# Batch 0 in half units of 256 and 320 tokens, with tiles of 64 tokens of two heads on 128 partitions

## The chip, the cores and the metric

The kernel runs on one core of a Trainium2 chip. The metric is the device time of one execution in microseconds. Five engines work side by side, each through its own list of instructions in order: TensorE (PE, with its weight loads as PEld), VectorE (DVE), ScalarE (ACT), GpSimd (POOL) and SyncE (SP), which issues most transfers.

## The reference, cut to what matters

```python
# q, k, v: (4, 8, 576, 64); M_prev: (4, 8, 64, 64); z_prev: (4, 8, 64); beta: (8,)
scores = q @ k.T / 8; scores[j > i] = -1e9
a = exp(scores - scores.max(-1)); a /= a.sum(-1) + 1e-09
local = a @ v
q_p = where(q > 0, q, exp(q) - 1) + 1
mem_out = (q_p @ M_prev) / ((q_p * z_prev).sum(-1) + 1e-6)
g = 1 / (1 + exp(-beta))
x = (g * mem_out + (1 - g) * local)          # to (2304 tokens, 512)
h = maximum(x @ w_in1, 0);  x = (s * h * h + b) @ w_out1
h = x @ w_in2;              out = (h * tanh(softplus(h))) @ w_out2
```

The attention is causal over 576 tokens of each batch, with a memory term. Two feed-forward layers of 512 x 2048 x 512 follow. The weights come as 64-bit numbers and are converted on the chip.

## The kernel before, in words

**A planner.** The program lists steps (`Plan.add`), each with an engine, an estimated duration, a priority, the buffers that it reads, writes or holds, and a function that issues the instructions. `Plan.order` runs an event simulation over these estimates and so fixes the order of the instructions of every engine; of the steps that are ready on an engine, the one with the lowest priority number goes first. A step that starts a buffer waits until its ring has a free place. The attention's TensorE steps carry a mode (1 for scores, 2 for the product with v), and among ready steps those of the current mode go first. Every transfer of attention and weights is a step of SP's queue.

**Attention in half units** (`pair`, from line 477). A half unit is a pair of heads (p = 0 to 3) of one batch and one group of tiles of 128 tokens: group TA (tiles 0 to 2, whose first 64 rows are padding: 320 tokens) or TB (tiles 3 and 4: 256 tokens). Batch 0's eight half units have priorities 7 x p for TA and 28 + 5 x p for TB (constants TIME_A, FIRST_B, TIME_B); the others start at 50. In one half unit, in the order of the list:

- transfers: q and z in rows (lines 514 to 517), q and k transposed (lines 521 and 524), M and v (line 656). A TA half of batch 0 keeps them in one of the four feed-forward weight buffers with r = 3, which aren't needed yet;
- the feature map: min with 0 on GpSimd (line 535), exp on ScalarE (536), max-add (537), product with z (538) and sum over 64 columns (539) on VectorE, then a gate (533) and a reciprocal (541) per row;
- scores on TensorE (line 571): contraction over 64 rows, so the two heads stand in the two row halves of the array;
- per tile and head: mask, row minimum of the negated scores on VectorE (line 581), the memory row q_p x gate of 64 columns on GpSimd (592), exp with row sums on ScalarE (589);
- gate and reciprocal of the row sums (533, 610), scaling of each tile (607; all on VectorE for batch 0's TA; for the rest tile 3 on GpSimd and tile 4 on VectorE);
- transposes on TensorE in blocks of 128 columns (line 630), copied from PSUM by ScalarE (635);
- the product PV with [M; v] on TensorE (line 652), contraction over 128 and each head in one column half. A batch-0 TA half then writes 256 tokens as a high and a low part straight into the first feed-forward block's input (lines 663 and 664), and every half copies its tokens (666) and stores them in `x_d` (668).

All PSUM results of the attention share the ring "a" of five banks.

**Weights.** `convert` takes one piece of 128 x 512 of a weight (of 64 pieces in the two layers, 32 in the first): a transfer of 512 KB (line 702), two ScalarE steps (707 and 713), a VectorE step that joins the bits (717), and the split into a high and a low part (724 and 727, both on VectorE). The constants CONV give each group of four pieces its priorities. `raw_buf` gives each piece one of a few landing buffers, some of them weight buffers that are not in use yet.

**The first feed-forward layer** goes in blocks of 256 tokens, with priority from 500 (RANK1), below all of the attention. Line 881 is its first product, line 957 the second. Block 0 needs `first_x` of all four TA halves; block 1 loads tokens 256 to 511 back from `x_d` (`load_x`, lines 902 to 904), which `x_needed` ties to the halves that cover them. Until the first matmul of line 881, the planner puts products of zeros (line 1389) where TensorE would be idle:

```python
    plan.fill = (7.0, 85.0, 0.12, zero_product)
    plan.fill_end = in_steps[0][0]
```

The half units and their places are listed near the end:

```python
    halves_ = [(0, p, TA, TIME_A * p, (nm, NR - 1), p % 2) for p, nm in enumerate(("wih", "wil", "woh", "wol"))]
    halves_ += [(0, p, TB, FIRST_B + TIME_B * p, x, p % 2) for p, x in enumerate((("woh", 2), ("wol", 2), ("wih", 3), ("wil", 3)))]
    for b, p, g, prio, *x in halves_[:H]:
        pair(b, p, prio, g, *x)
```

## Time and profile before

| | us |
|---|---|
| runs, median of 3 | 957.2 (957.04 to 958.82) |
| the profiled execution, its own time | 956.4 |
| its span, from first to last instruction | 954.6 |
| TensorE busy | 937.3 |
| VectorE busy | 776.0 |
| ScalarE busy | 641.5 |
| GpSimd busy | 220.7 |

How to read it: the profile is one execution recorded by the hardware profiler. Busy times are unions over an engine's instructions, so neighbouring instructions that overlap are not counted twice; the length given for a group of several instructions runs from the first start to the last end. Ends of matmuls are modelled. An idle time is put down to what released the instruction that ended it. The granted TensorE clock was 1.00 of full speed in all stretches.

### The profile page before, as it was taken

To read this page: it belongs to the slowest core of one execution; us is meant where nothing else is said; L and a number is where in the kernel's file an instruction comes from. 1 tells how busy PE (TensorE), PEld (TensorE's weight loads), DVE (VectorE), ACT (ScalarE), POOL (GpSimd) and SP (SyncE) were. 2 spreads that over 40 slices of the span, in tenths; PEclk is the share of its full clock that TensorE was granted. 3 is DMA by queue.
4 is the path that set the end of the run, shared out by engine and by line. 5 is a ranking of instruction groups with operands and counts; after the bars stand their busy time and mean duration, and the time that the engine had idled before them with its cause. 6 is when DMAs were issued, how large, how long until landed. Compare 5 with 4: busy or idle time off the path is not lost.

```text
span 954.6 us, 19318 instructions
## 1 busy us (share of the span) xinstructions
PE 937.3 (98%) x6594; PEld 862.0 (90%) x6594; DVE 776.0 (81%) x1886; ACT 641.5 (67%) x1393; POOL 220.7 (23%) x377
## 2 busy tenths in 40 slices
PE   7899999999999999999999999999999999999998
PEld 6677788878788999888899999999999999999998
DVE  6999989899978787568658998889957799577874
ACT  6899878777777476889757865557634476344652
POOL 4635445577663000000023400000000000000000
PEclk9999999999999999999999999999999999999999
DMA  9976757999996789988885658885786655775545
GB/s 236 311 201 176 235 162 224 266 267 265 283 257 198 221 282 308 291 301 274 291 289 165 206 184 266 303 278 177 234 285 218 209 163 191 259 226 199 170 139 178
DMA packets 148339, 224.11 MB, mean 235 GB/s; under 512 B 15120, under 2 KB 122640, under 8 KB 141328
## 3 DMA queue, kind: packets, MB, share of 16 engines
q1 hardware_dynamic: 141408, 174.63, 59.4%
q0 software_dynamic: 6688, 48.24, 15.3%
q8 instruction: 52, 0.85, 0.4%
q14 instruction: 47, 0.39, 0.1%
q10 hardware_dynamic: 144, 0.00, 0.0%
HBM read 159.39 MB, written 63.44 MB: 233 GB/s over the span
## 4 chain that ended last, share of the span: by engine, by line
PE 79%; DVE 4%; ACT 2%; DMA 1%; issue 1%; POOL 0%; DVEq 0%; POOLq 0%
PE bank L1112 20%; PE bank L1185 19%; PE bank L881 12%; PE bank L957 12%; PE bank L1188 5%; PE bank L652 4%; PE bank L630 4%; PE bank L571 3%; DMA stage<-wi_sums_d 1%; DVE S L740 1%; DMA qn<-in_qz 0%; DVE g L1118 0%; DVE woh L740 0%; POOL Pt L607 0%; DVE g L1150 0%
## 5 line engine op out<-in xcount | busy, mean ns | idle before, releaser
L1112 PE MATMUL bank<-wi,woh 128*128 128x384 f32 x477 | 112.5, 334 | 0.0
L1112 PE MATMUL bank<-wi,wol 128*128 128x384 f32 x483 | 105.9, 335 | 0.8 <-DVE wil L1118 0.6
L1185 PE MATMUL bank<-wol,S 128*128 128x256 f32 x756 | 102.3, 283 | 0.0
L1185 PE MATMUL bank<-woh,S 128*128 128x256 f32 x756 | 101.9, 283 | 0.0
L1185 PEld LDWEIGHTS bank<-wol,S 128*128 128x128 f32 x756 | 96.2, 192 | 0.0
L1185 PEld LDWEIGHTS bank<-woh,S 128*128 128x128 f32 x756 | 95.9, 192 | 0.0
L1112 PEld LDWEIGHTS bank<-wi,wol 128*128 128x128 f32 x483 | 85.6, 188 | 1.6 <-DVE wil L1118 0.9
L1112 PEld LDWEIGHTS bank<-wi,woh 128*128 128x128 f32 x477 | 85.2, 188 | 0.4
L589 ACT ACTIVATE Pt<-Pt,mx 128x64 f32<-128x64 f32 (+4 forms) x152 | 82.6, 564 | 1.8 <-DVE mx L581 1.8
L635 ACT COPY PT<-bank 128x384 f32<-128x384 f32 (+2 forms) x160 | 68.2, 491 | 22.4 <-PE bank L630 15.0
L607 POOL TENSOR_SCALAR Pt<-Pt,rs 128x448 f32<-128x448 f32 (+3 forms) x100 | 65.7, 676 | 39.2 <-DVE rs L610 26.8
L592 POOL TENSOR_SCALAR Pt<-ex,nm 128x64 f32<-128x64 f32 x152 | 60.2, 419 | 63.1 <-DVE nm L541 35.4
L630 PE MATMUL bank<-ident,Pt 128*128 128x128 f32 x444 | 62.5, 275 | 6.1 <-DVE Pt L607 1.7
L630 PEld LDWEIGHTS bank<-ident,Pt 128*128 128x128 f32 x444 | 49.5, 140 | 11.2 <-issue 3.4
L581 DVE CUSTOM_DVE_ANT_0 Pt<-bank,mask 128x64 f32<-128x64 f32 (+3 forms) x152 | 50.5, 373 | 8.0 <-PE bank L571 5.7
L739 ACT CAST woh<-stage 128x1024 fp32r<-128x1024 f32 (+2 forms) x42 | 37.2, 885 | 27.4 <-PE bank L1112 17.9
L740 DVE TENSOR_TENSOR woh<-stage,woh 128x1024 fp32r<-128x1024 f32 (+2 forms) x42 | 42.7, 1018 | 13.8 <-ACT woh L739 13.7
L1125 POOL TENSOR_SCALAR woh<-woh,sb 128x384 f32<-128x384 f32 (+1 forms) x6 | 5.5, 916 | 183.3 <-ACT woh L1124 183.3
L739 ACT CAST S<-g 128x384 fp32r<-128x384 f32 x56 | 28.7, 513 | 27.2 <-PE bank L1185 19.2
L1092 POOL DMA_DIRECT2D woh<-wo_split_d x13 | 6.9, 530 | 156.2 <-DVE g L1150 76.4
L881 PE MATMUL bank<-xh,wi 128*128 128x256 f32 x256 | 42.5, 292 | 0.0
L957 PE MATMUL bank<-gl,woh 128*128 128x256 f32 x256 | 41.5, 288 | 0.0
(331 smaller groups left out, 2491.1 us busy)
## 6 DMA issues: line engine op xcount, KB each, us to landing
woh<-wo_split_d POOLq DMA_DIRECT2D x13, 1024.0 KB, 5.6
wol<-wi_split_d POOLq DMA_DIRECT2D x12, 1024.0 KB, 5.2
wol<-wo_split_d POOLq DMA_DIRECT2D x11, 1024.0 KB, 5.2
stage<-in_w_in SPq DMA_DIRECT2D x21, 512.0 KB, 5.6
stage<-in_w_out SPq DMA_DIRECT2D x19, 512.0 KB, 4.7
stage<-wi_d SPq DMA_DIRECT2D x24, 384.0 KB, 5.1
stage<-wo_d SPq DMA_DIRECT2D x18, 512.0 KB, 3.7
wo_split_d<-high SPq DMA_DIRECT2D x32, 256.0 KB, 4.6
```

The costliest lines, as they stand in the source:

```text
L581: nc.vector.tensor_tensor_reduce(at_t(i, t, D + lo, D + hi), x.t[:, a:a + hi - lo], mask[:, SP - w + lo:SP - w + hi], -SCALE, mx.t[:, i, t ...
L589: nc.scalar.activation(at_t(i, t, D, w + D), at_t(i, t, D, w + D), AF.Exp, bias=mx.t[:, i, t + k:t + k + 1], scale=-1.0, accum_out=rs.t[:, ...
L592: add(POOL, 0.33, lambda i=i, t=t: nc.gpsimd.tensor_scalar(at_t(i, t, 0, D), ex.t[:, i, t - lo_t, :], nm.t[:, i, t - lo_t:t - lo_t + 1], 1 ...
L607: (nc.vector if e == DVE else nc.gpsimd).tensor_scalar(x, x, r, *((None, ALU.mult) if e == DVE else (1.0, ALU.mult, ALU.mult)))
L630: nc.tensor.transpose(ps.t[:, x, :], at_t(i, t, c * P, (c + 1) * P), ident)
L635: (nc.vector.tensor_copy if dve else nc.scalar.copy)(PT[i].t[:, x:x + n], ps.t[:, :n])
L739: lambda: (nc.scalar.copy if e == ACT else nc.vector.tensor_copy)(t[0](0), src()), r, [t[2], half], after)
L740: lo = two(add(DVE, dve_us(n), prio, lambda: nc.vector.tensor_tensor(t[0](1), src(), t[0](0).bitcast(F32), op=ALU.subtract), [*r, half], [ ...
L881: nc.tensor.matmul(ph, w_at(nm, r, cc)[:, o:o + P], x_at(x, cc), start=(begin and part == 0 and cc == 0), stop=(part == 2 and cc == NCC - ...
L957: nc.tensor.matmul(acc[ec // per].t[:, (ec % per) * n:(ec % per + 1) * n], w_at(nm, fc // FPR, fc % FPR)[:, ec * P:(ec + 1) * P], t(x)[:, ...
L1112: nc.tensor.matmul(ps.t[:, :H2], w[i // 4].t[:, j, kk, at_], x[kk].t[:, k], start=begin and part == kk == 0, stop=part == 2 and kk == 1, s ...
L1185: nc.tensor.matmul(acc[t].t[:, :DH], s.t[:, j, t * P:(t + 1) * P], x.t[:, k, q % 4], start=q == part == 0, stop=q == NQ2 - 1 and part == 2)
```

## The change

Batch 0's eight half units are no longer made by `pair` but by a new function `packed`. The first half has 256 tokens instead of 320, the second 320 instead of 256. In each there is one tile or two whose 128 partitions hold 64 tokens of one head and the same 64 tokens of the other: in the first half tokens 0 to 63 (width 64) and 192 to 255 (width 320, the last 64 keys masked), with one full tile per head between them (tokens 64 to 191); in the second half tokens 256 to 319, with two full tiles per head. Score products of a packed tile are 64 x 64 (line numbers as in the diff), those of a full tile 64 x 128 as before. A second half uses all five banks for scores in two turns, where before it used four.

q and z of the packed tiles and of the first halves are loaded for all pairs by `load_few` into one buffer, in rows of 64 numbers (256 bytes) per descriptor; second halves load the rest of their q. A table `gates` and a mask `steps` for the packed tiles are made at the start. Priorities change: first halves 6 x p, second ones 22 + 5 x p, the other batches from 44, the weight groups behind the first 2 to 4 earlier. The weight pieces with r < 2 use other landing buffers: four for r = 0, three for r = 1 (four before). The first half writes `x_d` up to token 256.

```diff
-TIME_A, FIRST_B, TIME_B, FIRST, TIME = 7.0, 28.0, 5.0, 50.0, 7.0
-CONV = ((-1.0, 3.0), (24.0, 2.0), (32.0, 2.0), (40.0, 2.0), (50.0, 3.0), (62.0, 3.0), (74.0, 3.0), (86.0, 3.0))
+TIME_A, FIRST_B, TIME_B, FIRST, TIME = 6.0, 22.0, 5.0, 44.0, 7.0
+CONV = ((-1.0, 3.0), (22.0, 2.0), (30.0, 2.0), (38.0, 2.0), (46.0, 3.0), (58.0, 3.0), (70.0, 3.0), (82.0, 3.0))
...
+E_PACKED = ('DDDD', 'PPDPD')
...
+    gates = at.tile([P, 2, H // 2, 6], F32, name="gates")
+    nc.vector.tensor_copy(gates[:, :, :, 2:].rearrange("p k a (h t) -> p (k a) h t", t=2),
+                          igate.rearrange("p k (a h) -> p (k a) h", h=2).unsqueeze(3).to_broadcast([P, H, 2, 2]))
+    for i in range(2):
+        x = slice(D * i, D * i + D)
+        nc.vector.tensor_copy(gates[x, :, :, :2], igate[x, :, i::2].unsqueeze(3).to_broadcast([D, 2, H // 2, 2]))
+    steps_ = at.tile([P, 3 * P], BF16, name="steps")
+    nc.gpsimd.memset(steps_[:, :2 * P], 0.0)
+    for i in range(2):
+        x = slice(D * i, D * i + D)
+        nc.gpsimd.tensor_copy(steps_[x, 2 * P:2 * P + D], mask[x, SP - P + D * i:SP - P + D * i + D])
+    nc.gpsimd.memset(steps_[:, 2 * P + D:], MASKED)
...
+    few, few_q, few_z, few_d = Buf(R["wih", 2], [P, 2048]), Buf(), Buf(), Buf()
+
+    def few_at(lo, n, *, s=1, rows=slice(0, P)):
+        return few.t[rows, lo:lo + n * D].rearrange("p (a s d) -> p a s d", s=s, d=D)
+
+    def load_few():
+        def get(us, prio, w, f):
+            attention_steps.append(add(DMA, us, prio, f, w=[w], keep=[few]))
+
+        def half_rows(i):
+            return slice(D * i, D * i + D)
+
+        for i in range(2):
+            for k in range(2):
+                get(0.25, 0.2, few_q, lambda i=i, k=k: nc.sync.dma_start(
+                    few_at(0, 16, s=4, rows=half_rows(i))[:, :, k], qz[0, i::2, (D, 0)[k]:(P, D)[k], (1, 3)[k]].rearrange("h p d -> p h d")))
+        for p in range(H // 2):
+            get(0.25, 0.3 + TIME_A * p, few_q if p == 0 else few_b[p], lambda p=p: nc.sync.dma_start(
+                few_at(0, 16, s=4)[:, p, 2:], qz[0, 2 * p:2 * p + 2, :, 2].rearrange("h p d -> p h d")))
+        get(0.5, 0.6, few_z, lambda: nc.sync.dma_start(few_at(16 * D, 8)[:, :, 0], qz[0, :, :, 0].rearrange("h p d -> p h d")))
+        for i in range(2):
+            get(0.15, 0.6, few_z, lambda i=i: nc.sync.dma_start(
+                few_at(24 * D, 4, rows=half_rows(i))[:, :, 0], qz[0, i::2, half_rows(i), 0].rearrange("h p d -> p h d")))
+        for i in range(2):
+            get(0.15, FIRST_B - 4.0, few_d, lambda i=i: nc.sync.dma_start(
+                few_at(28 * D, 4, rows=half_rows(i))[:, :, 0], qz[0, i::2, D:, 3].rearrange("h p d -> p h d")))
+
+    few_b = [few_q, *(Buf() for _ in range(3))]
...
+    def packed(p, half, prio, place, apart):
...
+        lo = half == 0
+        hs = slice(2 * p, 2 * p + 2)
+        nk, nb, n_s = (320, 3, 4) if lo else (S, 5, 5)
+        nq = 320
+        QN = nq + nk
+        VX = QN + (0 if lo else n_s * D)
+        all_, qk_in, q_in, v_in = Buf(R[place], [P, 2048]), Buf(), Buf(), Buf()
+        slots = (((0, 64), (192, 320), (64, 192, 0), (64, 192, 1)) if lo else
+                 ((0, 320), (64, 448, 0), (192, 576, 0), (64, 448, 1), (192, 576, 1)))
...
+        def q_all():
+            if lo:
+                return few_at(0, 16, s=4)[:, p]
+            return all_.t[:, QN:QN + n_s * D].rearrange("p (s d) -> p s d", d=D)
+
+        z_pair, z_both = (lambda: few_at(24 * D, 4)[:, p]), (lambda: few_at(16 * D + 2 * p * D, 2)[:, :, 0])
+
+        def fetch(us, f, w):
+            add(DMA, us, f, w=[w], keep=[all_])
+
+        if not lo:
+            fetch(0.5, lambda: nc.sync.dma_start(q_all()[:, 1:].rearrange("p (h t) d -> p h t d", t=2), qz[0, hs, :, 4:6].rearrange("h p a d -> p h a d")), q_in)
+        for i in range(2):
+            def load(i=i):
+                src = qk[0, 2 * p + i, rows(i)]
+                if lo:
+                    nc.sync.dma_start(all_.t[rows(i), :2 * nq].rearrange("p (a b) -> p a b", a=2),
+                                      src[:, D:][:, :2 * S].rearrange("p (a b) -> p a b", a=2)[:, :, :nq])
+                else:
+                    nc.sync.dma_start(all_.t[rows(i), :nq + nk], src[:, D + 256:SP + S])
+
+            fetch(0.0009 * (nq + nk), load, qk_in)
...
+        have = [few_q, few_b[p]] if lo else [q_in]
+        keep = [few] if lo else [all_, few]
+        if not lo:
+            add(POOL, 0.3 + 0.0032 * D, lambda: nc.gpsimd.tensor_copy(q_all()[:, 0], few_at(28 * D, 4)[:, p, 0]), [few_d], [q_in], keep)
+        add(POOL, 0.3 + 0.0032 * n_e, lambda: nc.gpsimd.tensor_scalar_min(ex.t, q_all(), 0.0), have, [ex], keep)
+        add(ACT, act_us(n_e), lambda: nc.scalar.activation(ex.t, ex.t, AF.Exp), [ex], [ex])
+        two(add(DVE, dve_us(n_e), lambda: nc.vector.scalar_tensor_tensor(ex.t, q_all(), 0.0, ex.t, op0=ALU.max, op1=ALU.add), [ex, *have], [ex], keep))
+        weighed = Buf()
+        for a, n in ((0, 2), (2, 2)) if lo else ((0, 1), (1, 4)):
+            def weigh(a=a, n=n):
+                x, y = q_all()[:, a:a + n], ex.t[:, a:a + n]
+                z = z_pair().to_broadcast([P, n, D]) if a == 0 else z_both()
+                if n == 4:
+                    x, y = (u.rearrange("p (h t) d -> p h t d", t=2) for u in (x, y))
+                    z = z.unsqueeze(2).to_broadcast([P, 2, 2, D])
+                nc.vector.tensor_tensor(x, y, z, op=ALU.mult)
+
+            two(add(DVE, dve_us(n * D), weigh, [ex, few_z, *have], [weighed], keep))
+        add(DVE, dve_us(n_e), lambda: nc.vector.tensor_reduce(nm.t[:, :n_s], q_all(), axis=mybir.AxisListType.X, op=ALU.add), [weighed], [nm], keep)
...
+        bank, scored = [Buf(R["a"], [P, 512]) for _ in range(2 if lo else 5)], Buf()
+        if lo:
+            where = {0: [(0, 64, 1, 192)], 1: [(0, 320, 0, 192)], 2: [(0, 192, 0, 0)], 3: [(0, 192, 1, 0)]}
+            turns = [([0, 1], [(2, 0, 0), (3, 0, 1), (1, 0, 0), (0, 0, 1), (0, 0, 0), (1, 0, 1)], 832)]
+        else:
+            where = {0: [(0, 320, 4, 0)], **{1 + 2 * i: [(0, 448, i, 0)] for i in range(2)},
+                     **{2 + 2 * i: [(0, 64, i, 448), (64, 576, 2 + i, 0)] for i in range(2)}}
+            turns = [([4, 0, 1], [(0, 0, 0), (3, 0, 1), (1, 0, 0), (0, 0, 1), (4, 0, 1), (2, 0, 0)], 832), ([2, 3], [(2, 1, 0), (4, 1, 1)], 512)]
+        for used, products, columns in turns:
+            def mm(products=products):
+                for s, k, i in products:
+                    q0, w, *full = slots[s]
+                    a, b, x, o = where[s][k]
+                    n = P if full else D
+                    nc.tensor.matmul(bank[x].t[:, o:o + b - a] if full else bank[x].t[rows(i), o:o + b - a],
+                                     all_.t[rows(i), q0:q0 + n], all_.t[rows(i), nq + a:nq + b], start=True, stop=True, skip_group_check=not full)
+
+            add(PE, 0.03 + columns * 0.00167, mm, [qk_in], [*(bank[x] for x in used), scored], [*(x for x, _ in Pt), mx, rs, all_], 1.0)
+            attention_steps[-1].mode = 1
+        for s in (0, 2, 3, 1) if lo else (0, 1, 3, 2, 4):
+            w, full = slots[s][1], len(slots[s]) > 2
+            for k, (a, b, x, o) in enumerate(where[s]):
+                def least(s=s, k=k, a=a, b=b, x=x, o=o, w=w, full=full):
+                    m = mask[:, SP - w + a:SP - w + b] if full else steps_[:, {(0, 64): 2 * P, (192, 320): D, (0, 320): 0}[slots[s]]:][:, :w]
+                    nc.vector.tensor_tensor_reduce(at(s, D + a, D + b), bank[x].t[:, o:o + b - a], m, -SCALE,
+                                                   mx.t[:, s:s + 1] if k else HUGE, ALU.add, ALU.min, mx.t[:, s + 8 * k:s + 8 * k + 1])
+
+                add(DVE, 0.14 + 0.00105 * (b - a), least, [bank[x]] + [mx_in[s]] * k, [Pt_in[s], mx_in[s]], [Pt[s][0], mx])
+            add(POOL, 0.33, lambda s=s: nc.gpsimd.tensor_scalar(at(s, 0, D), ex.t[:, s], nm.t[:, s:s + 1], 1.0, op0=ALU.mult, op1=ALU.mult),
+                [ex, nm], [Pt_in[s]], [Pt[s][0]])
+            add(ACT, 0.28 + 0.00083 * w, lambda s=s, k=k, w=w: nc.scalar.activation(
+                at(s, D, D + w), at(s, D, D + w), AF.Exp, bias=mx.t[:, s + 8 * k:s + 8 * k + 1], scale=-1.0, accum_out=rs.t[:, s:s + 1]),
+                [Pt_in[s], mx_in[s]], [Pt_in[s], rs_in[s]], [Pt[s][0], mx, rs])
...
+        for s in (0, 1, 2, 3) if lo else (0, 1, 3, 2, 4):
+            e, w = on(E_PACKED[half][s]), slots[s][1]
...
+        PT = [Buf(R["PT"], [P, 9, P]) for _ in range(1 if lo else 2)]
+        if lo:
+            groups = [(PT[0], 0, [(0, 0), (1, 0), (1, 1), (1, 2)]), (PT[0], 4, [(2, 0), (2, 1), (3, 0), (3, 1)])]
+        else:
+            groups = [(None, 0, [(0, c) for c in range(3)])]
+            groups += [(PT[i], 0, [(1 + 2 * i, c) for c in range(4)]) for i in range(2)]
+            groups += [(PT[i], 4 + a, [(2 + 2 * i, c) for c in range(a, b)]) for a, b in ((0, 3), (3, 5)) for i in range(2)]
...
+        def mm():
+            for c in range(nb):
+                for k in range(2):
+                    for i in range(2):
+                        x = pv.t[rows(i)]
+                        if lo and k == 0 and c == 0:
+                            dest, src = x[:, :384].rearrange("p (k n) -> p k n", k=2)[:, :, :D], PT[0].t[:, 0:2, rows(i)]
+                        elif lo and k == 0:
+                            dest, src = x[:, 192:256], PT[0].t[:, 1 + c, rows(i)]
+                        elif lo and c < 2:
+                            dest, src = x[:, 64:192], PT[0].t[:, 4 + 2 * i + c]
+                        elif not lo and k == 0 and c < 3:
+                            dest, src = x[:, :D], turned()[:, c, rows(i)]
+                        elif not lo and k == 1 and c < 4:
+                            dest, src = x[:, 64:320].rearrange("p (k n) -> p k n", k=2), PT[i].t[:, c:c + 5:4]
+                        elif not lo and k == 1:
+                            dest, src = x[:, 192:320], PT[i].t[:, 8]
+                        else:
+                            continue
+                        nc.tensor.matmul(dest, v_at(i, c), src, start=c == 0 and k == 0, stop=c == (2, nb - 1 - lo)[k], skip_group_check=k > 0)
...
+        if r < 2:
+            i = k % (4 - r)
+            return Buf(R["raw"], [P, 1024], I32) if i < 2 else Buf(R[("wil", 2) if i == 2 else ("wol", 1)], [P, 2048], I32)
...
-        edge = len(TA) * P - D
-        return [x_in[b, g] for b in range(B) for g in range(2) if b * S + g * edge < t0 + n and b * S + (edge, S)[g] > t0]
+        edge = [N1 if b == 0 else len(TA) * P - D for b in range(B)]
+        return [x_in[b, g] for b in range(B) for g in range(2) if b * S + g * edge[b] < t0 + n and b * S + (edge[b], S)[g] > t0]
...
+    load_few()
     for b, p, g, prio, *x in halves_[:H]:
-        pair(b, p, prio, g, *x)
+        packed(p, int(g == TB), prio, *x)
```

## Rows read from the trace of the kernel before

**Rows 1.** The page: busy time of each engine, and the chain that ended last
```profile
PE 937.3 (98%) x6594; PEld 862.0 (90%) x6594; DVE 776.0 (81%) x1886; ACT 641.5 (67%) x1393; POOL 220.7 (23%) x377
...
PE 79%; DVE 4%; ACT 2%; DMA 1%; issue 1%; POOL 0%; DVEq 0%; POOLq 0%
```

**Rows 2.** TensorE in order of time: start, us, what, count [idle before <-releaser]
```profile
9.20 3.26 PE L571 MATMUL bank<-wih 64*128 64x64 f32 x12 [3.46 <-DMA wih<-in_qk]
...
19.16 1.52 PE L652 MATMUL bank<-PT,wih 128*64 128x384 f32 x12
20.60 1.36 PE L571 MATMUL bank<-wil 64*128 64x64 f32 x12
...
29.08 0.82 PE L630 MATMUL bank<-ident,Pt 128*128 128x128 f32 x6
...
30.54 1.58 PE L652 MATMUL bank<-PT,wil 128*64 128x384 f32 x12
...
45.77 1.52 PE L652 MATMUL bank<-PT,wol 128*64 128x384 f32 x12
...
47.77 2.10 PE L571 MATMUL bank<-wol 64*128 64x448 f32 x12
49.80 1.22 PE L881 MATMUL bank<-xh,wi 128*128 128x256 f32 x8
...
57.81 2.17 PE L652 MATMUL bank<-PT,woh 128*64 128x256 f32 x20
...
103.90 0.66 PE L630 MATMUL bank<-ident,Pt 128*128 128x128 f32 x4 [1.26 <-POOL Pt L607]
104.31 0.72 PE L881 MATMUL bank<-xh,wi 128*128 128x256 f32 x4
```

**Rows 3.** Busy us by stretch: stretch, sum, PE, PEld, DVE, ACT, POOL, clock, DMA, GB/s
```profile
40.00:50.00 10.00, 9.04 (x62) 5.49 (x61) 10.00 (x35) 8.47 (x23) 5.31 (x5) 1.00 1.02 287
50.00:60.00 10.00, 9.60 (x83) 8.48 (x82) 9.93 (x31) 9.42 (x23) 3.73 (x7) 1.00 0.91 249
```

**Rows 4.** VectorE in order of time
```profile
10.63 0.56 DVE L538 TENSOR_TENSOR wih<-ex,wih 128x384 f32<-128x384 f32 x1
...
12.12 0.18 DVE L581 CUSTOM_DVE_ANT_0 Pt<-bank,mask 128x64 f32<-128x64 f32 x1
...
12.22 0.22 DVE L581 CUSTOM_DVE_ANT_0 Pt<-bank,mask 128x64 f32<-128x64 f32 x1
...
13.34 0.49 DVE L581 CUSTOM_DVE_ANT_0 Pt<-bank,mask 128x320 f32<-128x320 f32 x1
...
16.16 1.47 DVE L607 TENSOR_SCALAR Pt<-Pt,rs 128x64 f32<-128x64 f32 x6
...
29.54 0.55 DVE L537 SCALAR_TENSOR_TENSOR ex<-wol,ex 128x384 f32<-128x384 f32 x1
...
37.74 0.42 DVE L537 SCALAR_TENSOR_TENSOR ex<-woh,ex 128x256 f32<-128x256 f32 x1
...
102.73 0.68 DVE L904 TENSOR_TENSOR xl<-xr,xh 128x512 fp32r<-128x512 f32 x1
```

**Rows 5.** ScalarE in order of time
```profile
12.74 0.34 ACT L589 ACTIVATE Pt<-Pt,mx 128x64 f32<-128x64 f32 x1
...
15.28 0.19 ACT L589 ACTIVATION_READ_ACCUMULATOR Pt<-Pt,mx 128x1 f32 x1
...
17.33 1.63 ACT L635 COPY PT<-bank 128x384 f32<-128x384 f32 x4 [0.33 <-PE bank L630]
```

**Rows 6.** The page's groups: line engine op xcount | busy, mean ns | idle before
```profile
L607 POOL TENSOR_SCALAR Pt<-Pt,rs 128x448 f32<-128x448 f32 (+3 forms) x100 | 65.7, 676 | 39.2 <-DVE rs L610 26.8
L592 POOL TENSOR_SCALAR Pt<-ex,nm 128x64 f32<-128x64 f32 x152 | 60.2, 419 | 63.1 <-DVE nm L541 35.4
```

**Rows 7.** DMA queue of SP, 110 to 120 us: packets, MB, share of 16 engines
```profile
q1 hardware_dynamic: 1646, 1.37, 50.4%
```

**Rows 8.** The same queue, 620 to 640 us
```profile
q1 hardware_dynamic: 1862, 5.29, 77.9%
```

## What the change should do to the time

> **What bounds the kernel now.** I read the page's totals and its chain that ended last first [rows 1]: the chain runs 79% through TensorE, and TensorE is busy 98% of the span. The reader is to see in it that almost any microsecond of TensorE that is not useful work lengthens the run. Some busy time is not useful: until the first matmul of the feed-forward layer (line 881), the planner fills TensorE with products of zeros (line 1389). So I count: end = start of line 881 + useful TensorE work after it + idle after it. The third view, TensorE in order of time, gives the start: 49.80 us [rows 2]. After it idle is rare; the largest piece in the next 60 us is 1.26 us in front of 103.90 [rows 2], just before the second block of 256 tokens begins at 104.31 [rows 2].
>
> What sets the 49.80 us? The fourth view, engine load by stretch, shows VectorE at 9.93 to 10.00 of each 10 us between 40 and 60, ScalarE at 8.47 to 9.42, the transfers at 0.91 to 1.02 of the 16 engines, GpSimd at 3.73 to 5.31 [rows 3]. VectorE is the scarce engine while TensorE waits for the four first halves (called A, the other four B): their last product PV (line 652) starts at 45.77 and the layer 4.0 us later [rows 2]. The second block needs all four B halves, by a round trip over memory whose last VectorE step runs at 102.73 [rows 4].
>
> **VectorE, per half unit.** A goes from six tiles (two heads of widths 64, 192, 320; 1152 columns) to four (64, 320, 192, 192; 768 columns): instructions and columns both fall to exactly two thirds.
> - Masked minima (line 581): six run from 12.12 to 13.83 (13.34 + 0.49) [rows 4], less 0.08 of overlap with what follows 1.63 us; two thirds is 1.09: -0.54.
> - Scaling (line 607): six in 1.47 us [rows 4]: -0.49.
> - Feature map: 384 columns take 0.55, 256 take 0.42 [rows 4]. The max-add and the reduction fall by 0.13 each. The product with z becomes two of 128 columns, each about 0.29 on that line, less 0.08 of overlap: -0.05. Together -0.31.
> A: -1.34 us, four times -5.4.
> B goes from 4 x 64 to 5 x 64 feature columns and gains a tile of width 320: +0.07 twice, +0.14 for the split product (0.22 + 0.42 - 0.08 against 0.42), +0.42 for the minimum (0.49 [rows 4] less 0.07 of overlap); the new tile is scaled on GpSimd. B: +0.70, four times +2.8. **VectorE net -2.6 us.** The gate table costs a few copies once, before VectorE has any data: I take nothing, covered by the wait for the first weights; uncovered it is under 1 us.
>
> **ScalarE** follows: six exponentials with reads run from 12.74 to about 15.46, four copies take 1.63 [rows 5]; A has four and two wider ones: -0.9 and -0.5. **GpSimd** gains per B one copy and one more memory row of 64 columns (0.42 us each) and one scaling of 320 columns (under the mean of 0.68) [rows 6], 1.5 us; at 3.73 of 10 busy [rows 3] it has cover. Without it each B half would end up to 1.5 us later.
>
> **TensorE, per half unit.** Scores: 576 columns a row half in 1.36 us (A), 1024 in 2.10 (B) [rows 2], so 0.00165 us a column and 0.41 fixed. In A the packed tiles leave 192 + 320 + 320 = 832 columns in sequence: 1.78, +0.42. In B 320 + 448 + 64 + 512 = 1344: 2.63, +0.53. Transposes: six in 0.82 with 0.275 the length of one gives 0.109 pitch [rows 2]; A needs 8 for 12 (-0.44), B 21 for 18 (+0.33). PV: 768 columns in 1.52, 1152 in 2.17 [rows 2]; A 512: 1.09 (-0.43), B 1344: 2.49 (+0.32). So A -0.45, B **+1.18**. A lies ahead of the layer, in time filled with zeros, so it counts only through latency. Of B, the scores of two halves already run ahead of the layer (the second at 47.77 [rows 2]); if that stays, 4 x 1.18 - 2 x 0.53 = **+3.7 us** falls after the start, all on the path.
>
> **Transfers.** A's q, and z, come in 12 transfers of 256-byte pieces, ahead of the second weight piece, where the first pair had one transfer of 256 pieces of 1 KB. The first multiplication by z needs 2 x 4 x 128 + 256 + 1024 + 512 = 2816 of them. No row times a 256-byte piece alone. 1646 packets of 832 bytes on average took 0.504 x 160 us = 49 ns each [rows 7]; 1862 of 2841 bytes 134 ns [rows 8]. A line through both gives 25 ns at 256 bytes and 57 at 1 KB; 49 is the upper end. That is 4.4 us (to 8.6) over 16 engines against 0.9: the first multiplication, at 10.63 now [rows 4], comes 3.5 us (to 7.7) later. I take 25 ns, since the line rests on two rows and packets here fall with size. The scores come earlier instead (q, k of pair 0 move ahead, and TensorE waited 3.46 us for them at 9.20 [rows 2]), so minima and weight conversion fill VectorE; the chain behind the multiplication (by the lengths here some 0.9 us of sums, four memory rows of 0.42 on GpSimd [rows 6], scaling, transposes, copies) then puts the first PV near 20.4 for 19.16 [rows 2], an estimate: +1.3 (0 to +5.4). On VectorE, conversions stand behind the waiting multiplication, which nobody needs before the layer. On SP's queue there are 13 more issues at the start and one or two fewer per half; the ones behind them are weight pieces 2 and 3 and pair 1, whose bytes ahead of them are the same as before to 2%. The second eighth of the weights has three landing buffers instead of four: I take nothing, since VectorE is behind the transfers anyway; if it were not, I price it by the nearest hole in TensorE's backlog, the 1.26 us at 103.90 [rows 2].
> The Trainium skill ("DMA: Bandwidth & Descriptors", Specifications) wants at least 512 bytes per transfer for line rate. By it the lower figure would be too kind; no row here has such a piece by itself.
>
> **The start of the layer.** Pair 0: +1.3. Pair 1, from scores at 20.60 to PV at 30.54 [rows 2], loses 0.54 + 0.49 + 0.9 + 0.44 + 0.5 = 2.9. Pairs 2 and 3 come VectorE-paced, 15.2 us for both: -1.34 each. Sum -4.3. By VectorE's total alone it would be -5.4 (the range: 0 to -7.5 by the rivals). I take -4.8, the middle: 45.0 us.
>
> **Sum.** TensorE's side: -4.8 + 3.7 - 1.3 (the idle at 103 is filled by the backlog) = -2.4. The second block's side: all VectorE work ahead of it is 2.6 less. The later one decides, after which the kernel is as before: -2.5, with the planner's new order worth some +-1. Against the profiled execution's 956.4 (span 954.6 and 1.8 around it) that is 953.9; the runs' median, 957.2, is 0.8 above, so **954.7 us**. A measurement of this kernel can tell about 0.2%, 1.9 us.
>
> **Rivals.**
> - *The start gains more.* If A is paced by its own VectorE work alone (about 5.6 of the 7.6 us that a pair takes now), the start gains 7.5: -7.5 + 3.7 - 1.3 = -5.1, 952.1 us. For it: VectorE is full. Against: conversions and B halves share those gaps.
> - *Slow first loads.* With pair 0 late by 3.4 us, halfway to the upper bound, the start gains 2.7 and the sum is -0.3: 956.9 us (at 49 ns a piece, 5.4 late, 0.7 and +1.7: 958.9). For it: the transfers are as full as that [rows 3] in the first 60 us. Against: VectorE has other work then.
> - *The mixed shapes on TensorE (slower).* In B's first turn 64-row by 64-column products stand among 64 by 128 ones: three changes of shape. All score groups now keep one shape and show 0.41 us beyond their columns. If each change costs that, and different shapes don't run side by side (320 + 448 + 320 + 64 + 512 = 1664 columns, +0.53), a B half costs 3 x 0.41 + 0.53 = 1.76 more, four 7.0: -2.5 + 7.0 = +4.5, 961.7 us. It decides from 0.6 us per B half on. Five banks instead of four per B half, all the attention ring has, push the same way. Against: line 881, of another shape (128 x 128), starts at 49.80, right where the score group of 47.77 with its 2.10 us ends [rows 2].
> The Trainium skill ("TensorEngine Tiling (Array Packing)", Key Properties) says that a change of tiling mode drains the engine. By that rule this rival is the case; no row of before has such a change inside a group.
> That the change doesn't take place can't be: the list of half units calls the new function for all eight.
>
> **Chances.** The forecast 0.44 (its own range 952.0 to 956.5), larger gain 0.12, slow loads 0.20, mixed shapes 0.24. Faster by over 0.2% (below 955.3): most of the forecast (0.38), the larger gain, a little of the loads (0.02): 0.52. Within: 0.06 + 0.15 + 0.02 = 0.23. Slower (above 959.1): 0.22 + 0.03 = 0.25. The range reaches from below the larger gain, 950.5, into the mixed shapes, 961.0; what is left out is their upper half and some of the largest gains.
>
> **What would show it.** Line 881's successor starts near 45.0 us (right within 43 to 47); the four A score groups take about 1.8 us and the B groups 2.6 (mixed shapes: over 3.2); the first multiplication by z at about 14; B's PV about 2.5; TensorE idle around 100 us under 2 us and the second block at about 101.7. A start before 46 with an end not earlier would refute the sum: then B's TensorE work or idle behind the start ate it. A start after 48 would refute the VectorE reading.

## The result: slower, and where the time went

The changed kernel takes 965.16 us (median of 6 runs, 963.38 to 968.29), the kernel before 957.12 in the runs beside it: a ratio of 1.0083, 95% interval 1.0068 to 1.0099. The forecast of 954.7 had the wrong sign, and the time lies outside its range. The profiled execution of the changed kernel is the slowest of its six (968.29 us, span 966.5), so the traces differ by 11.9 us where the medians differ by 8.0.

The first view cuts the span where the first matmul of the layer begins (line 1129 now, 881 before): busy time of each engine (TensorE first) in the stretch ahead of it and behind it, first of the kernel before, then of the changed one.

```profile
0.00:49.80 49.80, 40.63 (x274) 30.89 (x274) 41.13 (x153) 36.88 (x108) 25.53 (x46) 1.00 0.99 273
49.80:954.60 904.80, 896.63 (x6322) 831.13 (x6320) 734.91 (x1735) 604.60 (x1287) 195.19 (x331) 1.00 0.74 233
```

```profile
0.00:50.99 50.99, 40.27 (x279) 29.84 (x279) 35.84 (x139) 31.46 (x86) 19.77 (x49) 0.90 0.97 242
50.99:966.50 915.51, 903.51 (x6390) 834.98 (x6388) 744.13 (x1743) 608.14 (x1297) 203.34 (x337) 1.00 0.73 231
```

Behind the start TensorE was busy 896.63 of 904.80 us, and is busy 903.51 of 915.51. So the 11.9 us of the traces are: start 1.2 later, 6.9 more work behind it, 3.8 more idle behind it. The prediction had -4.8, +3.7 and -1.3. All three terms failed in the same direction.

**Ahead of the layer.** TensorE in order of time:

```profile
6.97 3.16 PE L818 MATMUL bank<-wih 64*128 64x192 f32 x12 [6.97 <-DMA wih<-in_qk]
...
16.87 2.88 PE L818 MATMUL bank<-wil 64*128 64x192 f32 x12 [2.03 <-DMA wil<-in_qk]
...
21.12 1.91 PE L870 MATMUL bank<-ident,Pt 128*128 128x128 f32 x8
22.96 1.66 PE L900 MATMUL bank<-PT,wih 128*64 128x128 f32 x20
24.55 1.40 PE L818 MATMUL bank<-woh 64*128 64x192 f32 x12
...
41.15 3.66 PE L818 MATMUL bank<-woh 64*64 64x320 f32 x16
...
50.99 1.22 PE L1129 MATMUL bank<-xh,wi 128*128 128x256 f32 x8
...
112.81 0.98 PE L1129 MATMUL bank<-xh,wi 128*128 128x256 f32 x6 [0.58 <-ACT xh L1151]
```

The first scores start earlier than before, as forecast. Pair 0's group takes 3.16 us, twice as long as the same twelve products at 24.55, but it took 3.26 before, too [rows 2]. New is that pair 1's wait until 16.87 for q and k and take 2.88 us, and that they stand ahead of pair 0's transposes (line 870) and product PV (line 900). Three 10 us stretches (engines as above, then granted clock, DMA share, GB/s), first of the kernel before:

```profile
10.00:20.00 10.00, 10.00 (x61) 8.44 (x63) 9.65 (x34) 8.05 (x23) 3.78 (x8) 1.00 1.09 285
20.00:30.00 10.00, 8.35 (x73) 6.60 (x68) 9.90 (x46) 7.48 (x25) 7.20 (x14) 1.00 1.09 294
30.00:40.00 10.00, 9.79 (x74) 7.38 (x73) 9.51 (x36) 9.67 (x35) 5.30 (x9) 1.00 1.08 315
```

and of the changed one:

```profile
10.00:20.00 10.00, 7.97 (x41) 6.75 (x39) 7.05 (x26) 4.91 (x14) 2.99 (x6) 0.85 1.09 280
20.00:30.00 10.00, 8.29 (x63) 6.70 (x63) 7.02 (x30) 5.17 (x16) 4.67 (x7) 0.81 1.09 277
30.00:40.00 10.00, 9.99 (x94) 8.68 (x94) 8.32 (x39) 8.65 (x28) 5.24 (x12) 0.83 0.93 248
```

VectorE is busy 7.05, 7.02 and 8.32 here; it was 9.51 to 9.90 before. What the prediction took for the scarce engine now waits. The granted clock is 0.81 to 0.85: with levels of 1.2 and 2.4 GHz, 30 to 38% of each stretch at 1.2. TensorE had done nothing before 6.97 us, since the planner put no product of zeros ahead of the first scores (before, there were some from 2.80 us). What is everybody waiting for? The second weight piece on SP's queue and on ScalarE, in the kernel before:

```profile
3.63 0.47 SPq L702 DMA_DIRECT2D stage<-in_w_in  x1
```

```profile
11.62 0.66 ACT L707 ACTIVATE stage<-stage 128x512 f32<-128x512 f32 x1 [2.23 <-DMA stage<-in_w_in]
```

and SP's queue, then ScalarE, in the changed one:

```profile
3.26 3.13 SPq L698 DMA_DIRECT2D wih<-in_qz  x4
...
9.15 0.58 SPq L950 DMA_DIRECT2D stage<-in_w_in  x1
```

```profile
11.50 0.42 ACT L770 ACTIVATE ex<-ex 128x256 f32<-128x256 f32 x1 [3.97 <-POOL ex L769]
14.05 0.67 ACT L955 ACTIVATE stage<-stage 128x512 f32<-128x512 f32 x1 [2.13 <-DMA stage<-in_w_in]
...
15.16 0.33 ACT L834 ACTIVATE Pt<-Pt,mx 128x64 f32<-128x64 f32 x1
```

The eight issues of q and z run from 3.26 to 9.09 us, and what stands behind them on SP's queue is late: the second weight piece goes out 5.5 us later than before, is there at 14.05 for 11.62, and stands on ScalarE in front of pair 0's first exponential (15.16; 12.74 in [rows 5]). The chain of waits of the first 60 us, summed by line, puts the same loads first:

```profile
by line: DMA wih<-in_qz 18.8%; PE bank L818 17.9%; DMA wil<-in_qk 11.0%; PE bank L1638 9.0%; PE bank L870 8.9%; PE bank L1129 8.0%; DMA woh<-in_qk 5.7%; PE bank L900 5.2%; SPq L950 2.3%; SPq L748 2.3%; issue 1.7%; DVE rt L1187 1.2%; ACT rt 
```

In order of time it shows who waits for them:

```profile
3.26 5.87 DMA wih<-in_qz
...
9.15 0.58 SPq L950
...
10.25 6.57 DMA wil<-in_qk
...
16.84 5.43 DMA wih<-in_qz
...
22.29 3.40 DMA woh<-in_qk
```

It is SP's queue itself. The transfer issued at 3.26 lands at 9.13, and only then, at 9.15, does the second weight piece go out, eight places behind it in the queue. In the same way the issue at 16.84 follows the landing of the one at 10.25, and the issue at 22.29 that of the one at 16.84, each time eight places back. The kernel before does the same (there the issue at 9.17 follows the landing at 9.15): with eight transfers under way, the next issue waits for a landing. Before, the second weight piece was the sixth transfer of this queue; now it is the thirteenth. So a transfer more at the start costs its own issue, and it can cost a wait for a landing as well.

**B's scores** take 3.66 us a group. The forms of these products in the stretch 59 to 64 us (busy, mean ns) show why:

```profile
L818 PE MATMUL bank<-wih 64*64 64x320 f32 x4 | 1.5, 454 | 0.0
...
L818 PE MATMUL bank<-wih 64*128 64x448 f32 x4 | 1.0, 588 | 0.0
```

The two products of 448 columns share 1.0 us, so they run side by side; the two of 320, 64 columns of weights each, take 1.5 us: each stands alone, between products of another shape.

### The profile page after: what moved, and what is told of

Same layout as the page of the kernel before. It is cut to its first block, busy times and chain, and to the rows that moved or that the text cites. A ratio compares the mean times of both kernels' runs of the same rounds, so it can differ in the third digit from the quotient of the medians.

```text
span 966.5 us, 19436 instructions
## 1 busy us (share of the span) xinstructions
PE 943.8 (98%) x6666; PEld 864.8 (89%) x6666; DVE 780.0 (81%) x1881; ACT 639.6 (66%) x1381; POOL 223.1 (23%) x385
## 4 chain that ended last, share of the span: by engine, by line
PE 82%; DMA 7%; DVE 5%; ACT 4%; issue 1%; SPq 1%; POOL 1%; ACTq 0%; DVEq 0%; POOLq 0%
PE bank L1360 24%; PE bank L1433 18%; PE bank L1129 11%; PE bank L1205 10%; PE bank L1436 5%; PE bank L665 3%; PE bank L643 3%; PE bank L584 3%; PE bank L818 2%; ACT Pt L602 1%; DMA wih<-in_qz 1%; DMA woh<-wi_split_d 1%; DMA yr<-x_d 1%; PE bank L870 1%; PE bank L900 1%
## 5 line engine op out<-in xcount | busy, mean ns | idle before, releaser
L1360 PEld LDWEIGHTS bank<-wi,woh 128*128 128x128 f32 x525 | 92.9, 188 | 2.3 <-DMA woh<-wi_split_d 1.7
L1360 PEld LDWEIGHTS bank<-wi,wol 128*128 128x128 f32 x435 | 78.1, 188 | 0.3
L620 POOL TENSOR_SCALAR Pt<-Pt,rs 128x64 f32<-128x64 f32 (+3 forms) x96 | 61.5, 660 | 45.9 <-DVE rs L623 28.1
L648 ACT COPY PT<-bank 128x384 f32<-128x384 f32 (+2 forms) x120 | 50.6, 494 | 28.2 <-PE bank L643 20.2
L602 ACT ACTIVATE Pt<-Pt,mx 128x64 f32<-128x64 f32 (+4 forms) x120 | 66.4, 574 | 0.0
L605 POOL TENSOR_SCALAR Pt<-ex,nm 128x64 f32<-128x64 f32 x120 | 50.4, 443 | 35.6 <-DVE nm L554 20.3
L643 PE MATMUL bank<-ident,Pt 128*128 128x128 f32 x360 | 48.7, 274 | 1.7 <-POOL Pt L620 1.0
L594 DVE CUSTOM_DVE_ANT_0 Pt<-bank,mask 128x64 f32<-128x64 f32 (+3 forms) x120 | 41.5, 373 | 4.2 <-PE bank L584 3.1
L643 PEld LDWEIGHTS bank<-ident,Pt 128*128 128x128 f32 x360 | 40.4, 140 | 3.4 <-POOL Pt L620 2.4
L1129 PEld LDWEIGHTS bank<-xh,wi 128*128 128x128 f32 x256 | 34.5, 190 | 8.6 <-issue 4.0
```

The costliest lines, as they stand in the source:

```text
L602: nc.scalar.activation(at_t(i, t, D, w + D), at_t(i, t, D, w + D), AF.Exp, bias=mx.t[:, i, t + k:t + k + 1], scale=-1.0, accum_out=rs.t[:, ...
L605: add(POOL, 0.33, lambda i=i, t=t: nc.gpsimd.tensor_scalar(at_t(i, t, 0, D), ex.t[:, i, t - lo_t, :], nm.t[:, i, t - lo_t:t - lo_t + 1], 1 ...
L620: (nc.vector if e == DVE else nc.gpsimd).tensor_scalar(x, x, r, *((None, ALU.mult) if e == DVE else (1.0, ALU.mult, ALU.mult)))
L643: nc.tensor.transpose(ps.t[:, x, :], at_t(i, t, c * P, (c + 1) * P), ident)
L648: (nc.vector.tensor_copy if dve else nc.scalar.copy)(PT[i].t[:, x:x + n], ps.t[:, :n])
L1129: nc.tensor.matmul(ph, w_at(nm, r, cc)[:, o:o + P], x_at(x, cc), start=(begin and part == 0 and cc == 0), stop=(part == 2 and cc == NCC - ...
```

## The experiments

Each ratio is to runs of the kernel before taken beside that version (their medians are 957.4 to 958.4 us). The layer's start and the distance to the end are each read from a single profiled execution, and executions of one version differ by 1 to 6 us; the medians and intervals say what is clear of that. x7 and x10 load wrong rows of q and z, so they are probes and not kernels to use.

| run | median us (runs) | ratio, 95% interval | layer starts | from start to end of span |
|---|---|---|---|---|
| before | 957.12 (6) | | 49.80 | 904.8 |
| changed | 965.16 (6) | 1.0068 to 1.0099 | 50.99 | 915.5 |
| x1 same shapes together | 961.89 (7) | 1.0028 to 1.0060 | 48.10 | 911.5 |
| x2 zeros early | 964.18 (4) | 1.0038 to 1.0068 | 50.40 | 912.1 |
| x3 loads on ScalarE's queue | 969.00 (4) | 1.0090 to 1.0124 | 53.56 | 914.6 |
| x4 higher load costs | 964.31 (4) | 1.0044 to 1.0074 | 48.83 | 914.4 |
| x5 = x1 + x2 | 962.67 (6) | 1.0029 to 1.0063 | 48.45 | 913.2 |
| x6 x5, loads on GpSimd's queue | 963.18 (5) | 1.0034 to 1.0071 | 50.34 | 912.0 |
| x7 x5, two large transfers | 958.82 (10) | 0.9999 to 1.0026 | 44.90 | 912.7 |
| x8 x5 + x4 | 961.63 (10) | 1.0014 to 1.0043 | 45.63 | 914.8 |
| x9 x5, pair 0's pieces first | 963.29 (5) | 1.0047 to 1.0071 | 48.57 | 914.3 |
| x10 x7 in eight transfers | 961.87 (6) | 1.0029 to 1.0063 | 47.25 | 912.7 |
| x11 x9 with old due times | 968.53 (5) | 1.0101 to 1.0132 | 50.14 | 919.9 |
| x12 x5, weight piece first | 961.84 (5) | 1.0029 to 1.0059 | 49.56 | 910.5 |

### The mixed shapes

```diff
-turns = [([4, 0, 1], [(0, 0, 0), (3, 0, 1), (1, 0, 0), (0, 0, 1), (4, 0, 1), (2, 0, 0)], 832), ...
+turns = [([4, 0, 1], [(0, 0, 0), (0, 0, 1), (3, 0, 1), (1, 0, 0), (4, 0, 1), (2, 0, 0)], 832), ...
```

> The second halves' score groups with both 64 x 64 products first, so that one change of shape is left of three. Mixed shapes theory: the group takes 2.7 to 2.9 us instead of 3.66, 0.8 to 0.95 less four times, two of them ahead of the layer; the time falls by 2 to 4 us from the changed kernel's 965.2, to 961 to 963. Rival, the products with 64 output partitions are slow in themselves or don't run side by side in one bank: the group stays above 3.3 us and the time within 1.5 us of 965.2. Rival, first loads alone are the cause: the groups may shorten, but the layer's start stays at 51 and the time changes by under 2 us.

Both products of 64 by 64 now stand together. TensorE, the first such group and the layer's start:

```profile
39.47 2.79 PE L818 MATMUL bank<-woh 64*64 64x320 f32 x16
...
48.10 1.22 PE L1129 MATMUL bank<-xh,wi 128*128 128x256 f32 x8
```

and its forms, as above:

```profile
L818 PE MATMUL bank<-woh 64*128 64x448 f32 x4 | 1.0, 588 | 0.0
L818 PE MATMUL bank<-woh 64*64 64x320 f32 x4 | 0.8, 454 | 0.0
```

The two products of 320 columns now share 0.8 us, and the group takes 2.79 us for 3.66. The kernel falls by 3.3 us by the medians, 3.7 by the ratios; 4 x 0.87 is 3.5. Nothing but the order was changed, so that is its price. The Trainium skill ("TensorEngine Tiling (Array Packing)", Key Properties) says that a change of tiling mode drains the engine; the trace agrees, with 0.87 us for two changes fewer in a group; how much of it is a drain and how much the two products that stood alone is not separated. The same page (Gotcha 1: PSUM Pressure) says that different row tiles cannot use one PSUM bank at the same time. Here the two products write the two halves of one bank (partitions 0 to 63 and 64 to 127), and both together take 0.8 us, about as long as one of them when they stood alone (1.5 us for two); the measurement decides.

### Zeros, and the planner's costs

```diff
-plan.fill = (7.0, 85.0, 0.12, zero_product)
+plan.fill = (2.0, 85.0, 0.12, zero_product)
```

> The products of zeros may begin at 2 us of the plan instead of 7, so that 12 of them stand ahead of the first scores as in the kernel before; nothing else changes its order. Clock theory: the granted clock is 1.00 in 10 to 40 us (0.81 to 0.85 in the changed kernel's profile), the second pair's scores take 1.4 instead of 2.88 us, the layer starts at 47 to 49 instead of 50.99 and the time falls by 2 to 3 us. Rival, the loads pace the first halves whatever the clock: the layer's start moves by under 0.7 us and the time by under 1 us.

About 1 us by the medians, 2.9 by the ratios (the runs of before beside it were 1.0 us longer; the intervals touch), with the start at 50.40 for 50.99: the rival's side. The clock was not mended: TensorE works from 2.81 us on, yet the stretches of 10 to 30 us still show 0.82 and 0.84, with an idle time of 4.77 us in front of pair 1's scores. So the missing zeros alone did not bring the low clock; here TensorE's wait for late loads went ahead of it. Together with x1 it gives no more than x1 alone:

> Both 64 x 64 products first and the early products of zeros together. If the two effects are separate, the time is 961.9 less the 1.0 us of the zeros alone, 960 to 962, the layer's start 47 to 48.5. Rival, the zeros did nothing and were noise: 961.5 to 963. The base of the next three.

x4 only raises what the planner believes of the q and z transfers (0.25 to 0.75, 0.5 to 1.6, 0.15 to 0.45 us); x8 does that on top of x5.

> The planner's costs of the shared loads are tripled (0.75, 1.6 and 0.45 us instead of 0.25, 0.5 and 0.15), so that its order of all engines expects them later; the transfers are the same. Theory of engines blocked in their order by late loads: VectorE's idle time in 10 to 40 us (7.6 us in the changed kernel) falls below 4, the first pair's transposes no longer stand behind the second pair's scores, the layer starts at 47 to 49 and the time falls by 2 to 3 us. Rival, the loads are late whatever the order: the start stays within 1 us of 51.

> As the base, with the planner's costs of the shared loads tripled. If late loads block the engines in an order made for earlier ones, the start falls by 1 to 2 us and the time by 1 to 2 against the base. Rival, a new order only: within 1 us of the base, and a hole ahead of the second block as when the costs alone were changed (2.24 and 0.78 us).

In x4 pair 0's transposes and PV no longer stand behind pair 1's wait:

```profile
16.16 1.03 PE L870 MATMUL bank<-ident,Pt 128*128 128x128 f32 x8
17.62 2.03 PE L818 MATMUL bank<-wil 64*128 64x192 f32 x12 [0.42 <-DMA wil<-in_qk]
19.58 1.11 PE L900 MATMUL bank<-PT,wih 128*64 128x128 f32 x20
```

VectorE is idle 4.2 us between 10 and 40, near the 4 that was expected, and the granted clock is 1.00 there. The start comes 2 to 3 us earlier in both (48.83 for 50.99, 45.63 for 48.45), so late loads in an order made for earlier ones are a part of its delay. But little of it reaches the end, less than either expectation had: 0.9 us in x4, and 1.0 in x8 against x5, with intervals that overlap. In x8 the second block shows where it went, a wait of 2.40 us for its input:

```profile
105.16 0.68 PE L1129 MATMUL bank<-xh,wi 128*128 128x256 f32 x2 [2.40 <-ACT xh L1151]
```

### What makes the loads late: the queue, the pieces or the issues

The same transfers on other queues:

```diff
-get(0.25, 0.2, few_q, lambda i=i, k=k: nc.sync.dma_start(
+get(0.25, 0.2, few_q, lambda i=i, k=k: nc.scalar.dma_start(
```

> All loads of the shared q and z are issued from ScalarE's queue instead of SP's; the order of the work on TensorE is unchanged. Issue theory: SP issues the second weight piece near 3.5 us instead of 9.15, it lands at 9 to 11 instead of 14, the first pair's exponentials begin near 12 to 13 instead of 15.16, the layer starts at 47 to 49 and the time falls by 2 to 3 us. Rival, the transfers' bytes and small pieces set it, not their issue: the second weight piece lands after 13, the start moves by under 1 us. Rival, clock alone: no change of the start beyond 1 us while the clock stays low.

A miss. The issues keep ScalarE's own order: after the first at 1.44 us the next three wait until 6.27, behind the gate's activation, and the last of z goes out at 11.36. The kernel is 3.8 us slower than the changed one by the medians.

> As the kernel with the shapes and zeros mended, with the first eight shared loads issued from GpSimd's queue, which has nothing to do then; the order of the work is the same. Issue theory: SP issues the second weight piece near 3.5 us and it lands by 11 to 12 instead of 14, the second pair's q and k land by 14 instead of 17, the layer starts 2 to 3 us earlier, the time is 958 to 959.5. Rival, the transfers themselves are full and set it: the second pair's scores start after 16 as before and the time stays within 1 us of the base.

Here the eight issues went to GpSimd (`nc.gpsimd`). SP's queue is free of them, but GpSimd issues z's last transfers only at 8.40 and 9.73 us, and the first multiplication by z waits for its data until 18.88. Pair 1's q and k show that an early issue alone is not enough, either: they go out at 4.23 us instead of 10.35 (x5) and land no earlier (their scores start at 17.14, 16.72 in x5). The rival came out. Neither queue makes the loads early. The Trainium skill ("DMA: Bandwidth & Descriptors", Issuing engines are not separate DMA queues) says that spreading issues over engines saves only the issuing time, usually small beside the transfer. These two runs agree: nothing was gained, and an issue of q or z on SP takes 0.4 to 0.8 us where its transfer lands some 4 to 6 us after it.

Next the transfers themselves. x7 loads pair 0's q as 128 pieces of 1 KB in one transfer and z as 256 pieces of 1.5 KB in another (524 KB for 721); x10 has the pieces of x7 in eight transfers, as many as the changed kernel.

```diff
-few_at(0, 16, s=4, rows=half_rows(i))[:, :, k], qz[0, i::2, (D, 0)[k]:(P, D)[k], (1, 3)[k]]...
+few.t[:, lo:lo + 4 * D], qz[0, h, :, 1:5].rearrange("p a d -> p (a d)")
```

> As the base, with the same steps and order, but q and z of the shared buffer come in pieces of 1 KB and 1.5 KB: one transfer for pair 0's q instead of five, one for z instead of three, one for each later pair (numbers of other rows and heads stand in them, so the memory term is computed from wrong q and z). Small-pieces theory: the first multiplication with z comes at 10 to 11 instead of 12.6, the second pair's q and k land 2 to 3 us earlier, the layer starts at 44 to 46 and the time is 956.5 to 959. Rival, the order on the engines sets it and the loads matter little: start and time within 1 us of the base.

> The large-piece version (958.82 us, layer's start 44.90) with its 1 KB and 1.5 KB pieces, but in as many transfers as the changed kernel: 5 for pair 0's q and 3 for z instead of 1 and 1. As there, wrong rows and heads of q and z are loaded, so the memory term is computed from wrong data. If small pieces are the cause: time 958.5 to 960, start 45 to 46, as without the split. If the number of issues is the cause: the second weight piece is issued at about 9 us again, the start goes to 47 to 48.5 and the time to 961 to 962.5.

SP's queue and the layer's start, x7:

```profile
3.26 0.47 SPq L694 DMA_DIRECT2D wih<-in_qz  x1
3.77 0.43 SPq L701 DMA_DIRECT2D wih<-in_qz  x1
4.25 0.47 SPq L946 DMA_DIRECT2D stage<-in_w_in  x1
```

```profile
44.90 1.22 PE L1125 MATMUL bank<-xh,wi 128*128 128x256 f32 x8
...
104.96 0.98 PE L1125 MATMUL bank<-xh,wi 128*128 128x256 f32 x6 [0.58 <-ACT xh L1147]
```

and x10:

```profile
3.26 5.53 SPq L700 DMA_DIRECT2D wih<-in_qz  x8
8.84 0.58 SPq L952 DMA_DIRECT2D stage<-in_w_in  x1
```

```profile
47.25 1.22 PE L1131 MATMUL bank<-xh,wi 128*128 128x256 f32 x8
```

With two transfers the start is at 44.90, the forecast's 45.0. With the same pieces and bytes in eight it is at 47.25, so the number of transfers alone moves it by 2.35 us. The times agree, 958.82 and 961.87 us, with intervals that don't overlap. Of x10's 5.53 us for eight issues some 1.9 are waits for landings, the rest 0.4 to 0.5 us for each; the runs do not separate the two. x10 came out as the theory of the issues said.

With eight transfers of 256-byte pieces (x5) the start is at 48.45, 1.2 us later still. The times, 961.87 and 962.67 us, have the same interval, and in x10 the granted clock stays at 1.00 until 27 us, in x5 it is low from 9 us on. So what the small pieces cost, which the prediction had weighed, is not clear of the noise here. In x7 the first multiplication by z came at 12.13, not at 10 to 11.

x9 goes the other way: eight transfers ahead as before, but only pair 0's 896 of the 2816 pieces; the rest in seven more transfers behind pair 1's q and k.

```diff
+for n, (ps, us, prio) in enumerate(((slice(0, 1), 0.25, 0.2), (slice(1, 4), 0.5, TIME_A + 0.2))):
```

> Base is the version with the same-shape order and the early zeros (961.63 to 962.67 us in two calls; 961.6 to 963.3 profiled). Only the pieces of q and z that pair 0 needs are loaded ahead of the second weight piece: still 8 transfers, but 896 pieces of 256 bytes for 2816; those of the other three pairs follow after pair 1's q and k, in 7 more transfers. Everything is computed. If the number of small pieces is what delays the start: the first multiplication by z comes at about 10.5 to 11.5 us (12.6 in the changed kernel), the layer starts near 46 and the time is 959 to 960. If the number of transfers on SP's queue is what delays it: pair 0 gains little (the second weight piece is still issued at about 9.2), the 7 added issues of 4 to 5 us then delay pairs 1 and 2, the layer starts at 48 to 50 and the time is 962 to 964.

Start 48.57, 963.29 us, as the theory of the transfers' number has it. With a third of the pieces the eight issues still end at 8.68 us (9.18 in x5), and the second weight piece goes out at 8.72; the first multiplication by z gains 0.9 us (11.73 for 12.61). The base of this run and of x12 is x5, at 962.67 us; the 961.63 in the two expectations is the median of x8.

x12 moves one thing out from behind them, the second weight piece:

```diff
-add(DMA, 1.95, prio, ...
+add(DMA, 1.95, -0.5 if (layer, which, r, j) == (1, 'in', 0, 1) else prio, ...
```

> Base as before (same-shape order, early zeros; start 48.45, 961.63 to 962.67 us). The transfer of the second weight piece alone is issued ahead of pair 0's q, k and of the eight transfers of q and z, at about 1.2 us instead of 9.2; everything is computed. If the late second weight piece, standing on ScalarE in front of pair 0's exponentials, carries the delay: the start comes at 46 to 47 and the time is 960 to 961. If what carries it is that the eight issues make pair 0's z and pair 1's q and k late themselves: these still come after the eight issues, the start stays at 48 to 49.5 and the time at 961.5 to 963.

The start does not come earlier (49.56), as the second expectation had it. That does not clear the weight piece in front of ScalarE's exponentials, since the move displaced other loads. TensorE and SP show which:

```profile
9.97 1.89 PE L818 MATMUL bank<-wih 64*128 64x192 f32 x12 [2.32 <-DMA wih<-in_qk]
```

```profile
3.71 4.11 SPq L698 DMA_DIRECT2D wih<-in_qz  x4
...
10.44 1.46 SPq L705 DMA_DIRECT2D wih<-in_qz  x2
```

Pair 0's scores now wait for q and k until 9.97, z's last issue ends at 11.90. In these runs, whatever went first on this queue made the rest late.

### The due times

x11 gives x9 the planner's constants of the kernel before (first halves every 7 us, second halves from 28, the other batch from 50).

```diff
-TIME_A, FIRST_B, TIME_B, FIRST, TIME = 6.0, 22.0, 5.0, 44.0, 7.0
+TIME_A, FIRST_B, TIME_B, FIRST, TIME = 7.0, 28.0, 5.0, 50.0, 7.0
```

> The version that loads pair 0's pieces first, with the planner's due times (first and second half units, other batch, weight conversions) of the kernel before: 7, 28, 5, 50, 7 and conversions at 24 and on. If the earlier due times cause the rest of the loss behind the start (59.0 us from the layer's start to the second block in the large-piece version, against 54.5 before): the distance falls by 1 to 3 us and the time by 1 to 2. If the loss is the second halves' own TensorE work, dearer by 1.2 us each and more: the time changes by less than 1 us, or grows by up to 2 as the first halves move later.

It is 5.2 us slower than x9, more than either expectation had, so the changed kernel's earlier due times are a help and not the cause. No version here beats the kernel before; only x7 comes level with it, and it computes the memory term from wrong numbers.

## Why the prediction was wrong

**The start of the layer (-4.8; measured +1.2).** This step failed first. The prediction took VectorE as what sets the start and put the 13 more issues on SP's queue at nothing, since the bytes ahead of the weight pieces and pair 1 are the same to 2%. That holds for pair 1 with its own q and k. Ahead of the second weight piece the bytes are 29% more (1.77 MB for 1.38), and, which was not counted at all, twelve transfers stand there instead of five (eight of them q and z, where the prediction has 12). In a queue that issues in order and waits with eight under way, that number is what the runs showed: splitting two transfers into eight moved the start by 2.35 us and the time by 3.0 (x7 and x10). Its own condition came true ("a start after 48 would refute the VectorE reading").

The reckoned saving on VectorE is there: its instructions of the attention, added up by their lengths, take 199.9 us before and 197.4 in the changed kernel, 2.6 less, as forecast. It did not move the start, since VectorE waits: it is busy 35.84 of the 50.99 us ahead of the layer, and 41.13 of 49.80 before. That x7's start of 44.90 meets the forecast's 45.0 is therefore no proof of the VectorE terms; there, too, VectorE is busy only 34.70 us.

The first multiplication by z, forecast at about 14, came at 12.56. Yet pair 0's PV came at 22.96, 3.8 us late, much as the rival of slow first loads had it (3.4). That rival put it down to bytes in small pieces. The runs put it down to what stands in order behind the issues: pair 1's scores ahead of pair 0's transposes on TensorE (in x4, in the other order, PV is at 19.58), and TensorE at half its clock for part of the time. That the weight piece on ScalarE adds to it is likely by the order of time but not shown. And the rival let pair 1 follow at its old distance, where pair 1's own loads were late too.

**TensorE's work behind the start (+3.7; measured +6.9).** The B score groups are the rival of the mixed shapes: 3.66 us, above the 3.2 that was to show it, between the forecast's 2.63 and the rival's 4.39. Two groups lie behind the start, 2.1 us more than forecast. Put in order they take 2.79, and the stretch behind the start is still busy 5.0 us longer than before:

```profile
0.00:44.90 44.90, 37.83 (x293) 29.19 (x293) 34.70 (x135) 30.59 (x84) 20.77 (x47) 0.92 0.98 266
44.90:957.60 912.70, 901.63 (x6390) 834.77 (x6388) 745.46 (x1747) 608.76 (x1298) 204.57 (x338) 1.00 0.73 232
```

The terms as measured, 2 x (2.79 - 2.10) for scores, 1.3 for transposes as reckoned and 4 x (2.51 - 2.17) for PV (63.96 to 66.47 us in the changed kernel), give 4.1. The other 0.9 us are not attributed. A's scores were over-priced: 1.40 us for 1.78, since both row halves run side by side in A (192 + 64 + 320 = 576 columns, as before).

**Idle behind the start (-1.3; measured +3.8, and +2.9 in x7).** The hole at 103.90 [rows 2] did go, but 0.69, 0.58 and smaller ones took its place before and at the second block, which starts at 103.88 in x7 (forecast 101.7) with the layer's start as forecast. Later holes come on top that no step of the prediction looked at: 1.47 us at 349.08 and 1.53 us at 721.06 in the changed kernel. An early start is not worth its own length here: x8 starts 4.2 us before the kernel before and ends later. Why the idle time far behind grows, with the same lines there, stays open.

**What was right:** B's PV (2.51 for 2.49 us), VectorE's saving (2.6 us), the length of the two products with z (0.49 us for 0.50 in pair 0), and the named signs, two of which (the start after 48, score groups over 3.2 us) told which steps fell.

## What to carry to other kernels

Count transfers as well as bytes: where a queue issues in order, count the issues that stand ahead of each thing that the first microseconds need, see in the chain of waits whether an issue itself waits for an earlier landing (here for the one eight places back), and look at who waits for the last of them. In TensorE's row-packed products keep the same shape together, or the neighbours stop running side by side. And a gain at the start counts only when the wait that comes next is named too: here nearly all of it came back as work and waits behind the start.

## What was unexpected in the hardware

- An issue on SP costs much the same whatever it carries: about 0.6 us each for the four of 256 pieces of 256 bytes in the changed kernel (3.13 us with a wait of 0.6), 0.4 to 0.5 for those of 16 to 128 large pieces in x10 (5.53 us for eight, with waits of 1.9), 0.47 and 0.43 for the two of x7.
- With eight transfers under way, this program's next issue waits for the landing of the one eight places back: 9.15 after 9.13, 16.84 after 16.83, 22.29 after 22.27 us. Whether the chip or the program sets the eight is not shown.
- Products of 64 rows by 64 columns of weights run side by side with each other, in the same bank too (0.8 us for two of 320 columns), but alone when products of 64 by 128 stand between them (1.5).
- The granted clock fell in other places in each version: to 0.50 between 18 and 21 us in the changed kernel, and in x7, with early zeros, to 0.55 between 9 and 12. Of the ten runs of x7, the four at a mean clock of 1.000 took 958.2 us on average, the six at 0.996 to 0.998 took 959.6, with some overlap. Runs of the kernel before are at a lower clock, too (15 of the 22 beside x7; 958.3 us on average, 957.6 for the other seven), so it is not the change alone that brings it.
